# Linear-attention block with a routed FFN row: the kv blocks multiplied by wo on 32x32 tiles of the PE array, in program order

## The chip, the cores and the metric

One core of a Trainium2 chip runs the whole kernel as one launch. The time is device microseconds of that core. The engines are called PE (matmul; its weight loads are listed apart as PEld), DVE (the vector engine), ACT (the activation engine), POOL and SP; SP here only issues DMAs, and POOL does so too.

## What is computed

The input x has 2048 tokens of 1024 numbers. Everything is bf16 in memory.

```python
def _A_ref(x, wqkv, wo):                     # H = 32 heads of Dh = 32
    qkv = (x @ wqkv) ...                     # q, k, v by head
    phi = lambda t: jnp.where(t > 0, t + 1, jnp.exp(t)) + 1e-6
    pq, pk = phi(q), phi(k)
    kv = jnp.einsum("bhsd,bhse->bhde", pk, v)
    z = jnp.einsum("bhsd->bhd", pk)
    num = jnp.einsum("bhqd,bhde->bhqe", pq, kv)
    den = jnp.einsum("bhqd,bhd->bhq", pq, z)[..., None] + 1e-6
    return (num / den) ... @ wo
...
g = _sigmoid((x * gate_w).sum(-1, keepdims=True))
return g * a + (1 - g) * b
```

Here `a` is the attention above. `b` is x, with the output of a gated FFN (1024 to 3584 to 1024) added to the one token with the largest router value. Each head has its own 32x32 block kv, so for four heads (one "group" g of 128 channels) the product pk^T v is a 128x128 matrix of which only the four 32x32 blocks on the diagonal are wanted.

## The kernel before

The kernel has four stages. Sizes are partitions x columns.

- **Loading and first blocks** (lines 128 to 295): x arrives transposed (`xT`), the k and v weights as `wkv`, the q weights as `wq`. POOL writes constants: the identity `ident`, and `mask_bd` (lines 146 to 149), a 128x128 mask that is 1 on the four diagonal blocks.
- **The token loop** (lines 507 to 530), over 16 tiles of 128 tokens. For each tile four units `unit_KV` (line 222) of eight 128x512 matmuls each make k and v, and `unit_KVACC` (line 228) adds pk^T [v, 1] of all eight groups to three PSUM banks `kvacc`; its column 128 is z. Between them stand units of other work, as tables say (lines 33 to 36): units `unit_Q` (line 234), and pieces of the FFN. There are 32 Q units (8 groups g, 4 blocks j of 512 tokens); one is eight 128x512 matmuls into a bank of `ps_work`, which has four banks, and then phi: ACT computes `u`, then `e`, and DVE writes `pq_all` (lines 182 to 193). `Q_PER_T` (line 33) puts 15 Q units into the token loop. The FFN's gate and up weights are multiplied in steps; its down rows are added up on DVE (`yacc`, lines 438 to 443). The loads of the down rows stand between the loads of the second half's gate and up weights (`ffn_pieces`, line 447).
- **The middle** (lines 531 to 622). One Q unit, the last `unit_KVACC`, the end of the FFN (`yps`, `brow`), another Q unit. Then DVE copies z out (`zcol`, `zc`) and multiplies `kvacc` by the mask into `kvbd` (line 546). `den_group(0)` (line 561) makes the denominators of blocks j = 0 and 1 with sixteen 128x32-tile matmuls `dps`, which read `pq_all` of the first 16 Q units; ACT adds epsilon (`dn`), DVE takes the reciprocal (`rd`), and four DMAs, two on SP and two on POOL, spread it to `rdp`. Eight 128x128 transposes turn `kvbd` into `pt`, one DVE copy makes `kvT` of it (lines 604 to 607). A loop (lines 612 to 618) runs the last 14 Q units; after each of the last eight stands `unit_M(g)` (line 596), which multiplies group g's 128x128 `kvT` by wo: two 128x512 matmuls and two ACT copies into `m_sb`. After each Q unit stands one `norm_step` (line 586): DVE copies one row of `rdp` to all partitions (`stream_shuffle` into `rb`, four buffers), and POOL multiplies one 128x512 piece of `pq_all` by it. There are 32 such pieces, eight groups for each block j, in the order of j.
- **The output loop** (lines 625 to 649), over the 16 token tiles t: two banks of eight matmuls each of `pq_all` by `m_sb`, DVE combines them with the gated x (`ot`), a DMA writes the tile. Tile t needs all eight normalised pieces of block j = t // 4. In tile 0 also stands `den_group(1)`, for j = 2 and 3. `NORM_PER_T` (line 37) gives the norm steps after each tile: 2 after tile 0, none after 1 and 2, 3 after each later one until the pieces are used up.

What sets the order: the lines are recorded in the order of the code, and a scheduler then places them on each engine. Where `strict[0]` is true, the helper of line 72 ties each instruction of PE, DVE or ACT to the one before it, so that engine keeps the order of the code. In the kernel before it is false from line 297 on, except for a few lines. All instructions that go through that helper carry line 77 in the profile.

Of the kernel before, what the change touches and what calls it, by code (L numbers as in the profile page):

```python
# [13 lines left out]
BF = mybir.dt.bfloat16  # L14
F32 = mybir.dt.float32
I32 = mybir.dt.int32
U32 = mybir.dt.uint32
ALU = mybir.AluOpType
# [4 lines left out]
P = 128  # L23
S = 2048
D = 1024
# [3 lines left out]
NG = D // P  # L29
EPS = 1e-6  # L30
LN1EPS = math.log1p(EPS)
N_WARM = 6
Q_PER_T = {4: 2, 5: 1, 6: 1, 7: 2, 8: 1, 9: 1, 10: 2, 11: 1, 12: 1, 13: 2, 14: 1, 15: 0}
GU_AFTER = {(6, "end"), (7, 1), (7, "end"), (8, 1), (8, "end"), (9, "end"), (10, "end"), (11, "end")}
DOWN_STEPS = {9: (1, 1, 1, 1), 10: (1, 1, 1, 1), 11: (1, 1, 1, 1), 12: (1, 1, 1, 1, 1), 13: (1, 1, 1, 1), 14: (1, 1, 1, 1), 15: (1, 1, 1)}
FFN_DEPTH = 9
NORM_PER_T = [2, 0, 0, 3, 3, 3, 3, 3, 3, 3, 3, 3, 3, 3, 3, 3]


@with_exitstack  # L40
def kernel(
# [13 lines left out]
    nc = tc.nc  # L55
# [5 lines left out]
    const = ctx.enter_context(tc.tile_pool(name="const", bufs=1))  # L61
# [3 lines left out]
    ps_ffn = ctx.enter_context(tc.tile_pool(name="ps_ffn", bufs=1, space=PSUM))  # L65
# [4 lines left out]
    strict = [True]  # L70

    def in_order(engine, names):
        last = [None]

        def wrap(fn):
            def call(*a, **k):
                inst = fn(*a, **k)  # L77
                if last[0] is not None and strict[0]:
                    tc.add_manual_dep(inst.ins, last[0].ins.name, NOSYNC, reason="program order on this engine")
                last[0] = inst  # L80
                return inst

            return call

        return SimpleNamespace(**{n: wrap(getattr(engine, n)) for n in names})

    pe = in_order(nc.tensor, ["matmul", "transpose"])
    dve = in_order(nc.vector, ["memset", "tensor_copy", "tensor_scalar", "tensor_scalar_add", "tensor_tensor", "scalar_tensor_tensor",
                               "reciprocal", "max", "max_index", "tensor_reduce", "stream_shuffle"])
    sp = in_order(nc.sync, ["dma_start", "dma_start_transpose"])  # L90
    act = in_order(nc.scalar, ["activation", "copy"])
# [4 lines left out]
    kvbd = keep.tile([P, NG, P], BF)  # L96
# [45 lines left out]
    ident = const.tile([P, P], BF)  # L142
    make_identity(nc, ident[:])
    nc.scalar.dma_start(out=wrg_rows[0:8, :], in_=B_w_r.rearrange("(c p) -> c p", p=P))
    nc.scalar.dma_start(out=wrg_rows[8:16, :], in_=gate_w.rearrange("(c p) -> c p", p=P))
    mask_bd = const.tile([P, P], F32)
    nc.gpsimd.memset(mask_bd[:], 0.0)
    for i in range(4):
        nc.gpsimd.memset(mask_bd[32 * i : 32 * i + 32, 32 * i : 32 * i + 32], 1.0)
    nc.gpsimd.memset(mzc[:], 0.0)  # L150
    for hh in range(4):
        for g0 in range(4):
# [39 lines left out]
    def phi_evac(ps, out_ap):  # L192
        phi_dve(ps, phi_exp(ps), out_ap)
# [34 lines left out]
    def unit_KVACC(t):  # L228
        for g in range(NG):
            pe.matmul(kv_slot(g), lhsT=pk_t[t][:, g * P : (g + 1) * P], rhs=vt_t[t][:, g, :],  # L230
                             start=False, stop=False, skip_group_check=True)
        del pk_t[t], vt_t[t]

    def unit_Q(g, j):
        ps = ps_work.tile([P, 512], F32, tag="w")
        for c in range(KC):
            pe.matmul(ps[:], lhsT=wq[:, c, g * P : (g + 1) * P], rhs=xT[:, c, 512 * j : 512 * j + 512],
                             start=(c == 0), stop=(c == KC - 1))
        phi_evac(ps[:], pq_all[:, g, 512 * j : 512 * j + 512])
# [35 lines left out]
    for t in (2, 3):  # L275
        kv_open(t)
        for nb in range(2):
            pool, tag = (ps_t, "t") if t == 2 else (ps_work, "w")
            ps = pool.tile([P, 512], F32, tag=tag)
# [19 lines left out]
    for c in range(KC):  # L299
        for j in range(4):  # L300
            pe.matmul(rps[32 * j : 32 * j + 32, :], lhsT=wrg_pad[:, c, :], rhs=xT[:, c, 512 * j : 512 * j + 512],
                                  start=(c == 0), stop=(c == KC - 1), tile_position=(0, 32 * j))
# [173 lines left out]
    def ffn_step(n):  # L476
        for _ in range(n):
            ffn_flush()
            wt, comp = inflight.popleft()
            comp(wt)  # L480
            ffn_prefetch()
# [3 lines left out]
    def down_step(n):  # L485
        for _ in range(n):
            ffn_flush()
            if down["cur"] is None:
                down["cur"] = inflight.popleft()
            wt, comp = down["cur"]  # L490
            comp(wt, down["n"] % 2)
            if down["n"] % 2:
                down["cur"] = None
                ffn_prefetch()
            down["n"] += 1
# [11 lines left out]
    q_units = deque((g, j) for j in range(4) for g in range(NG))  # L507
    for t in range(4):
        unit_KVACC(t)
    for t in range(4, NT):  # L510
        for nb in range(4):
            unit_KV(t, nb)
            if nb == 1 and t > 4:
                unit_KVACC(t - 1)
            if (t, nb) in GU_AFTER:
                ffn_step(4)
            steps = DOWN_STEPS.get(t, ())
            if nb < len(steps):
                down_step(steps[nb])
        for i in range(Q_PER_T[t]):  # L520
            unit_Q(*q_units.popleft())
# [5 lines left out]
        if t == 5:  # L527
            router_part2()
        if (t, "end") in GU_AFTER:
            ffn_step(4)  # L530
# [2 lines left out]
    down_finish()  # L533
    gates()
    unit_Q(*q_units.popleft())

    zcol = keep.tile([P, NG], F32)
    for i in range(3):
        n = 3 if i < 2 else 2
        acc3 = kvacc[i][:, 0 : 129 * n].rearrange("p (g e) -> p g e", e=129)  # L540
        dve.tensor_copy(zcol[:, 3 * i : 3 * i + n], acc3[:, :, 128])
    dve.tensor_tensor(zc[:], mzc[:], zcol[:].unsqueeze(2).to_broadcast([P, NG, 32]), op=ALU.mult)
    for i in range(3):
        n = 3 if i < 2 else 2
        acc3 = kvacc[i][:, 0 : 129 * n].rearrange("p (g e) -> p g e", e=129)
        dve.tensor_tensor(kvbd[:, 3 * i : 3 * i + n, :], acc3[:, :, 0:128],
                                mask_bd[:].unsqueeze(1).to_broadcast([P, n, P]), op=ALU.mult)
    ph1.close()

    pb = ctx.enter_context(tc.tile_pool(name="pb", bufs=1))  # L550
    m_sb = pb.tile([P, NG, D], BF)
    wo = pb.tile([P, NG, D], BF)
    nc.sync.dma_start(out=wo[:], in_=A_wo.rearrange("(g p) n -> p g n", p=P))
    kvT = pb.tile([P, NG, P], BF)
    rdp = [pb.tile([P, 512], F32, name=f"rdp{i}") for i in range(2)]
    for r in rdp:
        nc.gpsimd.memset(r[:], 1.0)
# [1 line left out]
    ps_den = ctx.enter_context(tc.tile_pool(name="ps_den", bufs=3, space=PSUM))  # L559

    def den_group(pair):
        dps = ps_den.tile([P, 512], F32, tag="d")
        for g0 in range(4):
            for jj in range(2):
                for g1 in range(2):
                    g = 4 * g1 + g0
                    j = 2 * pair + jj
                    q = 2 * jj + g1
                    pe.matmul(dps[32 * q : 32 * q + 32, :], lhsT=zc[:, g, :], rhs=pq_all[:, g, 512 * j : 512 * j + 512],
                                     start=(g0 == 0), stop=(g0 == 3), tile_position=(0, 32 * q))  # L570
        dn = tmpb.tile([P, 512], F32, tag="dn")
        act.activation(dn[:], dps[:], ACTF.Identity, bias=eps_t[:, 0:1])
        rd = tmpb.tile([P, 512], F32, tag="rd")
        dve.reciprocal(rd[:], dn[:])
        for hh in range(4):
            eng = nc.sync if hh % 2 == 0 else nc.gpsimd
            eng.dma_start(out=rdp[pair][32 * hh : 32 * hh + 16, :], in_=rd[hh : P : 8, :])
        return rdp[pair]

# [6 lines left out]
    def norm_step(n):  # L586
        for _ in range(n):
            if not norm_units:
                return
            rd, g, j = norm_units.popleft()  # L590
            rb = tmpb.tile([P, 512], F32, tag="rb", bufs=4)
            dve.stream_shuffle(rb[:], rd[:], [8 * (j % 2) + g] * 32)
            sl = pq_all[:, g, 512 * j : 512 * j + 512]
            nc.gpsimd.tensor_tensor(sl, sl, rb[:], op=ALU.mult)  # L594

    def unit_M(g):
        for nh in range(2):
            ps = ps_den.tile([P, 512], F32, tag="d")
            pe.matmul(ps[:], lhsT=kvT[:, g, :], rhs=wo[:, g, 512 * nh : 512 * nh + 512], start=True, stop=True)
            act.copy(m_sb[:, g, 512 * nh : 512 * nh + 512], ps[:])  # L600

    rdA = den_group(0)
    unit_Q(*q_units.popleft())
    pt = ps_den.tile([P, NG, P], BF, tag="d")
    for g in range(NG):
        pe.transpose(pt[:, g, :], kvbd[:, g, :], ident[:])
    dve.tensor_copy(kvT[:], pt[:])
    normalise(rdA, 0)
    normalise(rdA, 1)
    g_m = 0  # L610
    nq_done = 0
    while q_units:
        unit_Q(*q_units.popleft())
        nq_done += 1
        if g_m < NG and nq_done > 6:
            unit_M(g_m)
            g_m += 1
        norm_step(1)
    while g_m < NG:
        unit_M(g_m)  # L620
        g_m += 1
    phq.close()

    fin = ctx.enter_context(tc.tile_pool(name="fin", bufs=3))
    for t in range(NT):
# [8 lines left out]
        for c0, cw in cols:  # L634
            ps = ps_work.tile([P, 512], F32, tag="w")
            for g in range(NG):
                pe.matmul(ps[:, 0:cw], lhsT=pq_all[:, g, t * P : (t + 1) * P], rhs=m_sb[:, g, c0 : c0 + cw],
                                 start=(g == 0), stop=(g == NG - 1))
# [6 lines left out]
        if t == 0:  # L645
            rdB = den_group(1)
            normalise(rdB, 2)
            normalise(rdB, 3)
        norm_step(NORM_PER_T[t])

# [29 lines left out]
```

## Time and profile before

| | |
|---|---|
| median of 3 runs | 257.94 us (257.4 to 258.1) |
| the profiled execution | 257.94 us, of which 256.4 us are its span |
| granted PE clock | 0.998 |
| PE busy | 249.9 us |
| DVE, ACT, POOL busy | 145.7, 126.9, 47.0 us |

The span is what the profile shows, from the first instruction to the last; 1.54 us of the execution's time lie outside it. A matmul's duration in the profile contains the time in which it passes through the array, and the next one starts before it ends: the 128x512 matmuls last 380 ns each, and start 216 ns after each other. So the cost of a row of matmuls is read from start to start. The profile's stages by time: the token loop ends at 162.8 us, the middle runs to 196.5 us, the output loop to the end.

### The profile page before, as it was taken

To read this page: it belongs to the slowest core of one execution; us is meant where nothing else is said; L and a number is where in the kernel's file an instruction comes from. 1 tells how busy PE (TensorE), PEld (TensorE's weight loads), DVE (VectorE), ACT (ScalarE), POOL (GpSimd) and SP (SyncE) were. 2 spreads that over 40 slices of the span, in tenths; PEclk is the share of its full clock that TensorE was granted. 3 is DMA by queue.
4 is the path that set the end of the run, shared out by engine and by line. 5 is a ranking of instruction groups with operands and counts; after the bars stand their busy time and mean duration, and the time that the engine had idled before them with its cause. 6 is when DMAs were issued, how large, how long until landed. Compare 5 with 4: busy or idle time off the path is not lost.

```text
span 256.4 us, 3781 instructions
## 1 busy us (share of the span) xinstructions
PE 249.9 (97%) x1400; PEld 116.6 (45%) x1426; DVE 145.7 (57%) x238; ACT 126.9 (49%) x202; POOL 47.0 (18%) x99
## 2 busy tenths in 40 slices
PE   8999999999999999999999999999999999999994
PEld 3444454454444444444444444444444444444443
DVE  0055024324155368996899723575986779954443
ACT  2195324545354444654445646466899732352210
POOL 6000001010000000000000000012997029960000
PEclk9999999999999999999999999999999999999999
DMA  6999992007999999879898100077000473454222
GB/s 189 307 330 189 238 315 76 0 3 239 354 348 348 340 336 344 255 227 328 270 438 276 4 0 0 4 234 237 1 3 0 121 233 119 164 179 149 84 82 82
DMA packets 47257, 47.71 MB, mean 186 GB/s; under 512 B 18364, under 2 KB 35140, under 8 KB 47176
## 3 DMA queue, kind: packets, MB, share of 16 engines
q1 hardware_dynamic: 46952, 47.34, 60.3%
q8 instruction: 11, 0.18, 0.3%
q0 software_dynamic: 256, 0.14, 0.2%
q14 instruction: 6, 0.05, 0.1%
q10 hardware_dynamic: 32, 0.00, 0.0%
HBM read 39.34 MB, written 8.40 MB: 186 GB/s over the span
## 4 chain that ended last, share of the span: by engine, by line
PE 95%; DMA 2%; issue 1%; SPq 1%; DVE 0%
PE ps L77 87%; PE kvacc L77 3%; PE first L77 2%; DMA wkv<-in_A_wqkv_dram 2%; PE dps L77 1%; PE rps L77 1%; SPq L77 1%; PE yps L77 0%; DVE ot L77 0%; PE pt L77 0%; PE xs_ps L77 0%; PE hps L77 0%; PE wps L77 0%
## 5 line engine op out<-in xcount | busy, mean ns | idle before, releaser
L77 PE MATMUL ps<-wkv,xT 128*128 128x512 bf16 x467 | 107.2, 380 | 0.6
L77 PEld LDWEIGHTS <-xT 128*128 128x128 bf16 x512 | 48.7, 98 | 58.9 <-issue 4.2
L77 PE MATMUL ps<-xT,wq 128*128 128x512 bf16 x249 | 58.0, 380 | 0.3
L77 ACT ACTIVATE u<-ps 128x512 f32<-128x512 f32 x60 | 35.8, 596 | 40.5 <-PE ps L77 37.2
L77 PE MATMUL ps<-m_sb,pq_all 128*128 128x512 bf16 (+1 forms) x259 | 55.2, 373 | 0.4 <-issue 0.2
L77 ACT ACTIVATE e<-u 128x512 f32<-128x512 f32 x64 | 40.4, 632 | 1.7
L77 PEld LDWEIGHTS <-pq_all 128*128 128x128 bf16 x264 | 25.7, 98 | 29.9 <-issue 0.4
L77 PEld LDWEIGHTS <-wq 128*128 128x128 bf16 x256 | 24.8, 98 | 30.4 <-issue 0.8
L594 POOL TENSOR_TENSOR pq_all<-pq_all,rb 128x512 bf16<-128x512 bf16 x32 | 36.0, 1160 | 8.7 <-DVE rb L77 8.7
L77 DVE SCALAR_TENSOR_TENSOR yacc<-wt,hcol,yacc 128x1024 f32<-128x1024 bf16 x27 | 34.6, 1281 | 3.7 <-DMA wt<-in_B_w_down_dram 3.1
L77 ACT CAST vt<-ps 128x512 bf16<-128x512 f32 x32 | 18.8, 588 | 34.5 <-PE ps L77 34.5
L77 DVE SCALAR_TENSOR_TENSOR pq_all<-ps,e 128x512 bf16<-128x512 f32 x32 | 21.6, 684 | 21.3 <-ACT e L77 21.3
L77 DVE SCALAR_TENSOR_TENSOR ot<-ps,gate,xg 128x512 bf16<-128x512 f32 (+1 forms) x33 | 23.7, 725 | 16.5 <-PE ps L77 15.0
L77 ACT ACTIVATE xg<-xt,omg 128x1024 f32<-128x1024 bf16 x16 | 18.2, 1147 | 25.9 <-DVE ot L77 25.9
L77 DVE SCALAR_TENSOR_TENSOR pk<-ps,e 128x512 bf16<-128x512 f32 x28 | 19.2, 687 | 20.1 <-ACT e L77 20.1
L77 DVE STREAM_SHUFFLE rb<-rdp 128x512 f32<-128x512 f32 x32 | 22.4, 736 | 0.0
L209 POOL MEMSET vt<- 128x8 bf16 x16 | 1.9, 137 | 105.7 <-PE kvacc L77 105.7
L77 PEld LDWEIGHTS <-pk 128*128 128x128 bf16 x128 | 8.5, 98 | 3.3 <-issue 0.4
L77 PE MATMUL kvacc<-vt,pk 128*128 128x129 bf16 x128 | 9.7, 221 | 0.1
L77 ACT CAST m_sb<-ps 128x512 bf16<-128x512 f32 x16 | 9.3, 583 | 0.0
L77 PE MATMUL first<-wkv,xT 128*128 128x512 bf16 x31 | 7.8, 396 | 0.6 <-DMA wkv<-in_A_wqkv_dram 0.6
L77 DVE RECIPROCAL rd<-dn 128x512 f32<-128x512 f32 x2 | 6.7, 3353 | 2.1 <-ACT dn L77 2.1
(96 smaller groups left out, 76.4 us busy)
## 6 DMA issues: line engine op xcount, KB each, us to landing
wt<-in_B_w_down_dram SPq DMA_DIRECT2D x14, 512.0 KB, 5.7
wt<-in_B_w_gate_dram SPq DMA_DIRECT2D x8, 512.0 KB, 7.0
wt<-in_B_w_up_dram SPq DMA_DIRECT2D x8, 512.0 KB, 8.8
xt<-xp SPq DMA_DIRECT2D x16, 256.0 KB, 2.7
out_dram<-ot SPq DMA_DIRECT2D x15, 256.0 KB, 2.0
wt<-in_B_w_gate_dram SPq DMA_DIRECT2D x8, 384.0 KB, 7.6
wt<-in_B_w_up_dram SPq DMA_DIRECT2D x8, 384.0 KB, 7.1
wkv<-in_A_wqkv_dram SPq DMA_DIRECT2D x8, 256.0 KB, 5.0
```

What stands on the lines that cost most here:

```text
L77: inst = fn(*a, **k)
L209: nc.gpsimd.memset(vt_t[t][:, :, 128:129], 1.0)
L594: nc.gpsimd.tensor_tensor(sl, sl, rb[:], op=ALU.mult)
```

## The change

- `Q_PER_T` gives 13 Q units to the token loop and not 15 (one fewer in tile 13, one fewer in tile 14). One more Q unit runs before `den_group(0)`, so that exactly the 16 units that it reads are before it, and the unit that stood right behind it moves into the loop, which now has 16 units.
- The mask goes: `kvbd` is a plain copy of `kvacc`.
- The eight 128x128 transposes become 32 products of one 32x32 block each with the identity (`unit_kvT`), into four banks. Four copies, two on ACT and two on DVE, make `kvT`.
- The sixteen 128x512 matmuls of `unit_M` become four batches of sixteen 32x32-tile matmuls with 512 columns. Row tile r of a batch writes bank r, column tile c its partitions 32c to 32c+31. The sixteen copies into `m_sb` go half to ACT and half to DVE. A batch needs four banks at once (three of `ps_den`, one of `ps_ffn`). The batches stand after units 4, 7, 10 and 13 of the loop.
- wo is loaded by eight DMAs of 32 partitions each, not by one.
- `den_group` and the whole loop are in program order on PE, DVE and ACT.
- The four `rdp` DMAs of `den_group(0)` are all issued by POOL.
- The loop has 8 norm steps and not 14: one after units 5, 6, 8, 9, 11, 12, 14 and 15. The output loop has 2, 3, 3 after tiles 0 to 2, and then 2 after each of tiles 3 to 10.

The lines that load and add the FFN's down rows are the same in both kernels.

```diff
-Q_PER_T = {4: 2, ... 12: 1, 13: 2, 14: 1, 15: 0}
+Q_PER_T = {4: 2, ... 12: 1, 13: 1, 14: 0, 15: 0}
+M_AFTER = {4: (0, 0), 7: (0, 1), 10: (1, 0), 13: (1, 1)}
-NORM_PER_T = [2, 0, 0, 3, 3, 3, 3, 3, 3, 3, 3, 3, 3, 3, 3, 3]
+NORM_PER_T = [2, 3, 3, 2, 2, 2, 2, 2, 2, 2, 2, 0, 0, 0, 0, 0]
...
     unit_Q(*q_units.popleft())
+    unit_Q(*q_units.popleft())
...
-        dve.tensor_tensor(kvbd[:, 3 * i : 3 * i + n, :], acc3[:, :, 0:128],
-                                mask_bd[:].unsqueeze(1).to_broadcast([P, n, P]), op=ALU.mult)
+        dve.tensor_copy(kvbd[:, 3 * i : 3 * i + n, :], acc3[:, :, 0:128])
...
-    nc.sync.dma_start(out=wo[:], in_=A_wo.rearrange("(g p) n -> p g n", p=P))
+    for hf in range(2):
+        for r in range(4):
+            nc.sync.dma_start(out=wo[32 * r : 32 * r + 32, hf, :, :], in_=wo_v[hf, r])
...
     def den_group(pair):
         dps = ps_den.tile([P, 512], F32, tag="d")
+        strict[0] = True
...
+        strict[0] = False
...
-            eng = nc.sync if hh % 2 == 0 else nc.gpsimd
+            eng = nc.sync if pair and hh % 2 == 0 else nc.gpsimd
...
+    def unit_kvT():
+        pt = four_banks("pt")
+        for hf in range(2):
+            for r in range(4):
+                for c in range(4):
+                    pe.matmul(pt[c][32 * r : 32 * r + 32, 32 * hf : 32 * hf + 32],
+                              lhsT=kvbd[32 * c : 32 * c + 32, 4 * hf + r, 32 * c : 32 * c + 32],
+                              rhs=ident[32 * c : 32 * c + 32, 32 * c : 32 * c + 32],
+                              start=True, stop=True, tile_position=(32 * c, 32 * r))
...
+    def unit_M(hf, nh):
+        pm = four_banks("pm")
+        for c in range(4):
+            for r in range(4):
+                pe.matmul(pm[r][32 * c : 32 * c + 32, :], lhsT=kvT[32 * r : 32 * r + 32, hf, c, :],
+                          rhs=wo[32 * r : 32 * r + 32, hf, c, 512 * nh : 512 * nh + 512],
+                          start=True, stop=True, tile_position=(32 * r, 32 * c))
+        for r in range(4):
+            eng = dve.tensor_copy if r % 2 else act.copy
+            eng(m_sb[:, 4 * hf + r, 512 * nh : 512 * nh + 512], pm[r][:])
...
     rdA = den_group(0)
-    unit_Q(*q_units.popleft())
-    pt = ps_den.tile([P, NG, P], BF, tag="d")
-    for g in range(NG):
-        pe.transpose(pt[:, g, :], kvbd[:, g, :], ident[:])
-    dve.tensor_copy(kvT[:], pt[:])
...
+    strict[0] = True
+    for i in range(len(q_units)):
         unit_Q(*q_units.popleft())
-        nq_done += 1
-        if g_m < NG and nq_done > 6:
-            unit_M(g_m)
-            g_m += 1
-        norm_step(1)
...
+        if i == 0:
+            unit_kvT()
+        if i in M_AFTER:
+            unit_M(*M_AFTER[i])
+        elif i >= 5:
+            norm_step(1)
+    strict[0] = False
```

More of the change, by code (lines that the diff above doesn't have):

```diff
@@ L32 @@
 N_WARM = 6
-Q_PER_T = {4: 2, 5: 1, 6: 1, 7: 2, 8: 1, 9: 1, 10: 2, 11: 1, 12: 1, 13: 2, 14: 1, 15: 0}
+Q_PER_T = {4: 2, 5: 1, 6: 1, 7: 2, 8: 1, 9: 1, 10: 2, 11: 1, 12: 1, 13: 1, 14: 0, 15: 0}
 GU_AFTER = {(6, "end"), (7, 1), (7, "end"), (8, 1), (8, "end"), (9, "end"), (10, "end"), (11, "end")}
+M_AFTER = {4: (0, 0), 7: (0, 1), 10: (1, 0), 13: (1, 1)}
 DOWN_STEPS = {9: (1, 1, 1, 1), 10: (1, 1, 1, 1), 11: (1, 1, 1, 1), 12: (1, 1, 1, 1, 1), 13: (1, 1, 1, 1), 14: (1, 1, 1, 1), 15: (1, 1, 1)}
 FFN_DEPTH = 9
-NORM_PER_T = [2, 0, 0, 3, 3, 3, 3, 3, 3, 3, 3, 3, 3, 3, 3, 3]
+NORM_PER_T = [2, 3, 3, 2, 2, 2, 2, 2, 2, 2, 2, 0, 0, 0, 0, 0]
 @with_exitstack
@@ L145 @@
     nc.scalar.dma_start(out=wrg_rows[8:16, :], in_=gate_w.rearrange("(c p) -> c p", p=P))
[L146 to L149, printed above, removed]
     nc.gpsimd.memset(mzc[:], 0.0)
@@ L551 @@
     m_sb = pb.tile([P, NG, D], BF)
-    wo = pb.tile([P, NG, D], BF)
-    nc.sync.dma_start(out=wo[:], in_=A_wo.rearrange("(g p) n -> p g n", p=P))
-    kvT = pb.tile([P, NG, P], BF)
+    wo = pb.tile([P, 2, 4, D], BF)
+    wo_v = A_wo.rearrange("(hf r c e) n -> hf r e c n", hf=2, r=4, c=4)
+    for hf in range(2):
+        for r in range(4):
+            nc.sync.dma_start(out=wo[32 * r : 32 * r + 32, hf, :, :], in_=wo_v[hf, r])
+    kvT = pb.tile([P, 2, 4, 32], BF)
     rdp = [pb.tile([P, 512], F32, name=f"rdp{i}") for i in range(2)]
@@ L594, in norm_step @@
             nc.gpsimd.tensor_tensor(sl, sl, rb[:], op=ALU.mult)
[L596 to L600, printed above, removed]
-    rdA = den_group(0)
-    unit_Q(*q_units.popleft())
-    pt = ps_den.tile([P, NG, P], BF, tag="d")
-    for g in range(NG):
-        pe.transpose(pt[:, g, :], kvbd[:, g, :], ident[:])
@@ L607, with four_banks @@
-    dve.tensor_copy(kvT[:], pt[:])
+    def four_banks(name):
+        banks = [ps_den.tile([P, 512], F32, tag="d", name=f"{name}{r}") for r in range(3)]
+        banks.append(ps_ffn.tile([P, 512], F32, tag="f", name=f"{name}3"))
+        return banks
+    def unit_kvT():
[8 more added lines that the diff above has]
+        for c in range(4):
+            eng = dve.tensor_copy if c % 2 else act.copy
+            eng(kvT[:, :, c, :], pt[c][:, 0:64].rearrange("p (h d) -> p h d", h=2))
@@ new lines, in unit_M @@
+    def unit_M(hf, nh):
+        pm = four_banks("pm")
+        for c in range(4):
+            for r in range(4):
[5 more added lines that the diff above has]
+            eng(m_sb[:, 4 * hf + r, 512 * nh : 512 * nh + 512], pm[r][:])
@@ L608 @@
+    rdA = den_group(0)
     normalise(rdA, 0)
     normalise(rdA, 1)
-    g_m = 0
-    nq_done = 0
-    while q_units:
+    strict[0] = True
+    for i in range(len(q_units)):
         unit_Q(*q_units.popleft())
-        nq_done += 1
-        if g_m < NG and nq_done > 6:
-            unit_M(g_m)
-            g_m += 1
-        norm_step(1)
-    while g_m < NG:
-        unit_M(g_m)
-        g_m += 1
+        if i == 0:
[4 more added lines that the diff above has]
+            norm_step(1)
```

## The prediction

> **What bounds the kernel.** I read the page's busy shares and slices first, then PE's waits, then the chain of work, then the timeline of the middle.
>
> ```profile
> span 256.4 us, 3781 instructions
> ...
> PE 249.9 (97%) x1400; PEld 116.6 (45%) x1426; DVE 145.7 (57%) x238; ACT 126.9 (49%) x202; POOL 47.0 (18%) x99
> ...
> PE   8999999999999999999999999999999999999994
> ```
>
> PE is full in every slice but the first and last. Its waits are three rows, all in the first 8 us or far too small:
>
> ```profile
> PE warm_ps L77 <- PEq L664: 1.0, 1, 1.0
> PE first L77 <- DMA wkv<-in_A_wqkv_dram: 0.6, 2, 0.3
> PE ps L77 <- issue: 0.2, 1, 0.2
> ```
>
> So the time is PE's instructions laid end to end. A change can win only by taking work from PE, and loses every wait that it gives PE. The chain in order of time has what the changed pieces cost PE (columns: start, us, what):
>
> ```profile
> 58.17 0.30 PE xs_ps L77 x9
> ...
> 167.09 0.97 PE dps L77 x16
> 168.06 0.54 PE ps L77 x2
> 168.60 0.45 PE pt L77 x8
> ```
>
> `pt` is the eight transposes, 56 ns each. `xs_ps` is nine tiny products, each with its own weight load: 33 ns apiece, the fastest pace of such pairs here. `dps`, on 128x32 tiles, runs at about 57 ns: four column tiles share a stream of 216 ns. The sixteen `ps<-wo,kvT` matmuls cost 16 x 0.216 = 3.46 us.
>
> What a Q unit needs after its last matmul is seen in the timeline of the middle (start, duration, engine):
>
> ```profile
> 174.26 0.60 ACT L77 ACTIVATE u<-ps 128x512 f32<-128x512 f32 x1 [0.47 <-PE ps L77]
> 174.89 0.63 ACT L77 ACTIVATE e<-u 128x512 f32<-128x512 f32 x1
> 175.55 0.69 DVE L77 SCALAR_TENSOR_TENSOR pq_all<-ps,e 128x512 bf16<-128x512 f32 x1 [0.95 <-ACT e L77]
> ...
> 177.93 0.73 DVE L77 STREAM_SHUFFLE rb<-rdp 128x512 f32<-128x512 f32 x1
> ...
> 178.82 2.29 POOL L594 TENSOR_TENSOR pq_all<-pq_all,rb 128x512 bf16<-128x512 bf16 x2 [4.96 <-DVE rb L77]
> ```
>
> u starts 0.20 after the unit's end (matmuls from 194.35 plus 8 x 0.216 give 196.08; the u there starts at 196.28). With 0.60, 0.63, 0.69 and the gaps, `pq_all` is written **2.2 us** after PE has finished the unit. A normalisation takes 0.73 on DVE, 0.16 of hand-over and 1.15 on POOL: about **2.0 us** more. Before, all of this is hidden.
>
> **The change, part by part.** The sum is made against the profiled execution, 257.94 us (span 256.4 plus 1.54 outside); that is also the median.
>
> *Moved Q units.* 2 x 1.73 us leave the token loop and come back in the middle: 0. DVE's last `yacc` ends at 144.9, 18 us before `yps`, and PE there has four banks, so an earlier tile 14 (by 1.73) meets DVE free. 0 (up to +0.5 if DVE were still behind).
>
> *Mask.* `kvbd` copies instead of products (0.52 and 0.41 us on DVE) stay hidden behind two Q units: 0. POOL's five mask memsets lie in its first 4 us; PE's first transposes wait for x: 0.
>
> *Down rows.* The built order of SP's loads is the same in both kernels: 0.
>
> *wo in eight DMAs.* Before, one DMA is issued at 166.84, 3.45 after the last `kvacc`, and lands in 9.9 us. Eight issues of about 0.4 to 0.6 us take 4 us; the first batch stands 16 us after that `kvacc`. About 3 us of margin even if it all lands at 3.45 + 9.9: 0. Without the margin each us late is a us on PE.
>
> *rdp by POOL.* Four issues of 0.5 us and 3.9 us to landing: about 6 us after `rd`. The first shuffle stands behind the sixth unit's phi, about 10 us after `rd`: 0.
>
> *Order, first place: `dps`.* Before, the scheduler put `dps` 14 matmuls behind the 16 units that it reads. Now it follows unit 16 at once, in program order, and its sixteenth matmul reads that unit's `pq_all`. With U the end of unit 16: `pq_all` at U + 2.2; PE has done 15 `dps` at U + 0.09 + 15 x 0.0575 = U + 0.95. Behind the waiting matmul the whole loop queues on PE. **+1.25 us** (0.9 to 1.6).
>
> *Second place: the last normalisations of j = 0.* Before, block 0's eight pieces were done six units before the loop's end. Now the steps after units 14 and 15 are the last two, and in program order each shuffle stands behind its unit's phi. With T the end of the last Q unit: piece 6 is shuffled from T - 1.73 + 2.2 = T + 0.45, and is through POOL at T + 2.5, at PE by T + 2.6. In the built order PE has seven matmuls of tile 0 (six pieces, one of the second bank) ahead: T + 1.5. **+1.1 us** (0.7 to 1.6). Piece 7 is ready at T + 2.2 + 2.0 + 0.1 = T + 4.3; PE, delayed, has eight more matmuls to do first: 2.6 + 1.73 = T + 4.35. So 0 more.
>
> *Third place: j = 1 at tile 4.* Before, 14 of the 16 pieces of j = 0 and 1 were through in the loop; now 8, and tile 4's last three are shuffled only behind tile 2's `ot`. DVE, in the built order: two `ot` and one shuffle until T + 6.9, the reciprocal (3.35 us in its row) until T + 10.2, two `ot` (0.74) and two shuffles until T + 12.9, two `ot` until T + 14.3, then three shuffles (0.65 apart) ending at 15.0, 15.7, 16.3. POOL needs 1.15 for each: 16.35, 17.5, 18.65. PE: tile 0 and `dps` until T + 5.95, 15 matmuls of tile 1 until 9.2, tiles 2 and 3 (3.46 each) until 16.1; piece 7 of tile 4 is wanted at 17.6, and comes at 18.75. **+1.15 us** (0.4 to 1.8). Later blocks have four tiles for eight pieces at two a tile: 0.
>
> *Products.* A batch at the pace of `xs_ps` is 16 x 0.033 = 0.53, and about 0.2 for changing tile shape (around `dps` PE loses 0.09 ahead and 0.06 to 0.28 behind). 4 x 0.73 = 2.9 for 3.46: **-0.55**. Bounds: all sixteen together, 4 x (0.216 + 0.15) = 1.5: -2.0; at the pace of `dps`, 64 x 0.0575 + 0.8 = 4.5: +1.0; no two row tiles together, 64 x 0.216 = 13.8: +10.4. No row here has a row tile. I take the issue pace: with both tilings the 216 ns stream is shared by up to sixteen, and something under 57 ns then sets the pace. The copies go half to DVE, which then has 5 x 0.69 + 2 x 0.74 = 4.9 us of work in each 5.9 us of loop (three units and a batch): 0.
>
> *Blocks turned.* 32 x 0.033 + 0.2 = 1.25 for 0.45: **+0.8** (0 to +1.7). The copies are wanted four units later.
>
> The Trainium skill speaks of these products, beside the numbers above. "TensorE: Matmul & The Clock Gate", Measured speedup vs the span model, gives 660 ns for sixteen 32x32 tiles of 512 columns: an estimate from that page is 2.64 us for the four batches, which would make the sum 0.26 lower. Against the change speaks "TensorEngine Tiling (Array Packing)", Key Properties: "Changing tiling mode (not just tile) drains the TensorE". The gaps around `dps` agree in kind, at 0.06 to 0.28 us; the change makes ten such switches more, and no run here shows them for row tiles.
>
> **Sum.** 1.25 + 1.1 + 1.15 - 0.55 + 0.8 = +3.75: **261.7 us**. The work taken from PE is small; the waits that program order and the later normalisation give it are not.
>
> **Rivals.**
>
> - *The row tiles run all at once* (faster). Place: the four batches. Price: -2.0 (and the blocks turned at +0.3). It decides only if the three waits sum to under 0.9 us; with 0.6 it gives 257.94 - 1.7 + 0.6 = 256.8. For it: 512 columns are one stream however many tiles share it, as `dps` shows for four. Against: the waits are in the built order itself, 3.5 us by the rows above. With its products and waits at their low ends (2.0) the time is 258.2. Chance of faster by over 0.3%: 0.09.
> - *It moves little* (the down rows aren't changed; what PE gains it gives back): within 0.3%, 257.2 to 258.7. Needs waits of about 2 us with the cheapest products. Chance 0.11.
> - *Row tiles run one after another* (much slower): +10.4 instead of -0.55: 272.6. For it: consecutive products of a batch share a column tile, and nothing here shows row tiles overlapping. Against: nothing shows them excluding each other. Chance 0.05.
> - *wo comes late.* The first two batches need its first half, 12.5 us after issue at the latest. At the pace before it lands in 5; at a quarter of that pace in 20, 7 us late: about 269. For it: each DMA now writes 32 partitions. Against: the rows that it moves are the same 2 KB. Chance 0.04.
> - The forecast, slower by 1 to 7 us: 0.71.
>
> 0.3% (0.77 us) is about what this kernel's measurement can tell from no change. Faster 0.09, within 0.11, slower 0.80. The range leaves out the last two rivals above and the faster one below: all low ends give +0.3 (258.2), the high ends without it 1.6 + 1.6 + 1.8 + 1.0 + 1.7 = +7.7; I take 258.0 to 265.0.
>
> **What would show it.** PE's waits gain rows: `dps` for DVE `pq_all` (about 1.25 us, once), a weight load of `pq_all` for POOL at tile 0 (1.1) and at tile 4 (1.15). `pm` costs about 0.7 us a batch, start to start, `pt` 1.25. It would be wrong if PE shows no such waits, if a batch is near 0.35 or over 1.2 us, or if PE waits for wo.

## The result, and the profile after

The changed kernel takes **259.44 us** (median of 4 runs, 259.17 to 259.56) against 257.88 before (257.4 to 258.1): a ratio of **1.0061**, interval 1.0044 to 1.0079. That is slower by 1.56 us, where +3.75 was forecast. The profiled execution took 259.56 us; 258.0 of it are its span (256.4 before), at a granted clock of 1.0.

Of the page: the span, the busy times, and PE's forty slices.

```profile
span 258.0 us, 3927 instructions
...
PE 248.5 (96%) x1471; PEld 114.7 (44%) x1498; DVE 150.4 (58%) x247; ACT 124.2 (48%) x196; POOL 47.7 (18%) x96
...
PE   7999999999999999999999999899998999999994
```

PE has 1.4 us less to do, and the span is 1.6 us longer. Two slices in the middle, near 165 and 197 us, have fallen from 9 to 8. PE's waits (columns: us in total, times, the longest) say why:

```profile
PE ps L78 <- POOL pq_all L596: 1.2, 2, 0.7
PE dps L78 <- DVE pq_all L78: 1.1, 1, 1.1
PE warm_ps L78 <- PEq L682: 1.0, 1, 1.0
PE first L78 <- DMA wkv<-in_A_wqkv_dram: 0.8, 1, 0.8
PE ps L78 <- issue: 0.3, 2, 0.2
```

The last three rows were there before, of about the same size. The first two are new. The weight loads have a new row as well, 2.5 us at the same two stops: a weight load stops first, and the matmul behind it is then late by the rest.

```profile
PEld L78 <- POOL pq_all L596: 2.5, 3, 1.2
```

PE's timeline of the middle (start, duration, what, the idle time before it) has all the changed pieces:

```profile
159.94 0.64 PE L78 MATMUL yps<-yacc,ones_f 128*32 128x256 f32 x8
160.74 3.40 PE L78 MATMUL ps<-xT,wq 128*128 128x512 bf16 x15 [0.16 <-issue]
164.07 1.04 PE L78 MATMUL dps<-pq_all,zc 128*32 128x512 bf16 x15
166.21 0.38 PE L78 MATMUL dps<-pq_all,zc 128*32 128x512 bf16 x1 [1.10 <-DVE pq_all L78]
166.52 1.90 PE L78 MATMUL ps<-xT,wq 128*128 128x512 bf16 x8
168.35 0.29 PE L78 MATMUL pt<-ident,kvbd 32*32 32x32 bf16 x32
168.81 6.85 PE L78 MATMUL ps<-xT,wq 128*128 128x512 bf16 x31 [0.16 <-issue]
175.59 0.43 PE L78 MATMUL pm<-wo,kvT 32*32 32x512 bf16 x16
175.96 5.35 PE L78 MATMUL ps<-xT,wq 128*128 128x512 bf16 x23
```

Fifteen `dps` start right behind the sixteenth Q unit; the sixteenth `dps` is held up for 1.10 us, and all of the loop stands behind it. A batch of sixteen products lies between 175.59 and the next Q unit's start at 175.96: **0.37 us**. (31 and 23 records where 32 and 24 matmuls ran: a record is missing in each, so the gap at 168.81 is a matmul without a record; the `issue` rows of PE's waits, here and before, are such gaps.) The start of the output loop, and its later stop:

```profile
196.37 1.67 PE L78 MATMUL ps<-m_sb,pq_all 128*128 128x512 bf16 x7
198.77 2.17 PE L78 MATMUL ps<-m_sb,pq_all 128*128 128x512 bf16 x9 [0.73 <-POOL pq_all L596]
201.09 1.05 PE L78 MATMUL dps<-pq_all,zc 128*32 128x512 bf16 x16
202.07 11.83 PE L78 MATMUL ps<-m_sb,pq_all 128*128 128x512 bf16 x53
214.35 40.12 PE L78 MATMUL ps<-m_sb,pq_all 128*128 128x512 bf16 x190 [0.45 <-POOL pq_all L596]
```

Both stops are on the chain that ended last (columns: start, us, what); before, this stretch of the chain was PE alone, but for some 0.2 us of issue, most of it a matmul without a record:

```profile
195.47 0.64 ACT e L78
...
196.14 0.63 DVE pq_all L78
196.77 0.72 DVE rb L78
...
197.55 1.17 POOL pq_all L596
...
198.77 2.19 PE ps L78 x9
```

It is the path that the prediction described for the second place: phi of the last but one unit, its shuffle, POOL's product, and then PE.

**Where the time went.** Start to start on PE, profile against profile:

| stage | before | after | difference | forecast |
|---|---|---|---|---|
| start of `yps`, less the two Q units moved (3.46) | 163.32 | 159.94 | +0.08 | 0 |
| `dps` start to next Q unit | 0.98 | 2.45 | +1.47 | +1.25 |
| blocks turned, with the change of tile shape | 0.45 | 0.33 | -0.12 | +0.8 |
| products with wo: 16 x 0.216; 4 x (0.37 + 0.10) | 3.45 | 1.88 | -1.57 | -0.55 |
| tile 0 to `dps` (after has one matmul more, 0.22) | 3.55 | 4.72 | +0.95 | +1.1 |
| second `dps` to the next matmul (before: from 200.06 to 201.04, see below) | 0.98 | 0.98 | 0 | 0 |
| from there to the last matmul (after has one matmul fewer, 0.22) | 52.00 | 52.42 | +0.64 | +1.15 |
| behind the last matmul | | | +0.15 | 0 |

The sum is +1.60, the difference of the spans. The 0.10 is what PE loses ahead of the smaller tiles: the eight Q matmuls from 166.52 end their starts at 168.25, and `pt` begins at 168.35. For the two rows on the second `dps` the profile before needs care:

```profile
201.26 51.77 PE L77 MATMUL ps<-m_sb,pq_all 128*128 128x512 bf16 x243 [0.16 <-issue]
```

Here 243 records stand for 248 matmuls, and the gap ahead of them is one without a record: it started 0.22 earlier, at 201.04. In the run with both mends, below, all 248 have records, and the first starts 0.98 after `dps`, as in the kernel after.

### The profile page after: what moved, and what is told of

Same layout as the page of the kernel before. It is cut to its first block, busy times and chain, and to the rows that moved or that the text cites. A ratio compares the mean times of both kernels' runs of the same rounds, so it can differ in the third digit from the quotient of the medians.

```text
span 258.0 us, 3927 instructions
## 1 busy us (share of the span) xinstructions
PE 248.5 (96%) x1471; PEld 114.7 (44%) x1498; DVE 150.4 (58%) x247; ACT 124.2 (48%) x196; POOL 47.7 (18%) x96
## 4 chain that ended last, share of the span: by engine, by line
PE 90%; DMA 2%; ACT 2%; POOL 1%; issue 1%; DVE 1%; SPq 0%
PE ps L78 82%; PE kvacc L78 3%; PE first L78 2%; DMA xnat<-in_A_x_dram 2%; POOL pq_all L596 1%; ACT e L78 1%; PE rps L78 1%; ACT u L78 1%; DVE rb L78 1%; PE dps L78 1%; DVE pq_all L78 1%; SPq L78 0%; PE pm L78 0%; ACT m_sb L78 0%; PE pst L78 0%
## 5 line engine op out<-in xcount | busy, mean ns | idle before, releaser
L78 PE MATMUL ps<-xT,wq 128*128 128x512 bf16 x250 | 57.4, 379 | 0.5 <-issue 0.3
L78 DVE CAST r_bf<-rps 128x512 bf16<-128x512 f32 x1 | 0.7, 692 | 12.1 <-PE rps L78 12.1
L78 PE MATMUL ps<-wt,xs_pad 128*32 128x512 bf16 (+1 forms) x128 | 7.5, 355 | 0.0
```

## The experiments

**The theory after the result:** the waits are as forecast, in their places and near their sizes (3.06 us together), and stand in the order and in the number of norm steps, not in the tiles; the tiles give 1.7 us. (The expectations below have 0.86 us for the third wait. That is 0.22 too much, the matmul without a record.) **The rival:** the tiles give little, and the waits are smaller than their rows suggest because something else of the change pays for them (the two moved Q units, the order). If the first holds, each wait must go when its own cause is mended, and the tiles must cost 1.7 us when they are taken back. The first seven runs below and the last change the kernel after; the four between them put the tile products into the kernel before.

### One more Q unit ahead of the first dps

```diff
+    strict[0] = True
+    unit_Q(*q_units.popleft())
     rdA = den_group(0)
...
-    for i in range(len(q_units)):
-        unit_Q(*q_units.popleft())
-        if i == 0:
+    for i in range(16):
+        if i:
+            unit_Q(*q_units.popleft())
+        if i == 1:
             unit_kvT()
```

> One Q unit is moved ahead of dps (17 and not 16 before it), and the turning of the blocks behind the next one; all else as in the changed kernel. Theory (the change loses time in three waits of PE, 1.47 us at dps, 0.95 at tile 0, 0.86 at tile 4): the dps wait goes, 259.4 - 1.4 = 258.0. Rival (the middle is bound by DVE and ACT, so that PE waits somewhere else instead): 259.2 to 259.6, with a new wait in the loop. Rival (program order itself costs): 259.4, no row changes but the one.

Measured: **258.17 us**, ratio to before 0.9999 (0.9982 to 1.0017). The `dps` row is gone from PE's waits, the POOL row is as it was:

```profile
PE ps L78 <- POOL pq_all L596: 1.2, 2, 0.7
PE warm_ps L78 <- PEq L685: 1.0, 1, 1.0
PE first L78 <- DMA wkv<-in_A_wqkv_dram: 0.7, 1, 0.7
```

So the first place is worth 1.3 us by the medians (259.44 less 258.17), and it is the distance between the last phi and its reader. The output loop does not change with it: from tile 0 to PE's end it takes 58.1 us in both.

### A norm step after every unit from the sixth on

```diff
         if i in M_AFTER:
             unit_M(*M_AFTER[i])
-        elif i >= 5:
+        if i >= 5:
             norm_step(1)
```

> Three more norm steps in the loop (after each unit from 5 on, so 11 and not 8); all else as in the changed kernel. Theory of the three waits: piece 7 of block 0 is through three units before the loop's end, and block 1 has three pieces more done by then, so both waits for POOL go: 259.4 - 0.95 - 0.86 = 257.6. Rival (DVE cannot take three more shuffles of 0.73 us in the loop): PE waits for a bank in the loop, 259 or more.

Measured: **257.69 us**, ratio 0.9998 (0.9976 to 1.002). With eleven norm steps in the loop, not eight, POOL is no longer among what PE waits for; the `dps` row stays:

```profile
PE dps L78 <- DVE pq_all L78: 1.1, 1, 1.1
PE warm_ps L78 <- PEq L682: 1.0, 1, 1.0
PE first L78 <- DMA wkv<-in_A_wqkv_dram: 0.6, 1, 0.6
```

The second and the third place are worth 1.75 us together by the medians (1.59 in the table), and both go with three norm steps more in the loop, those that the change leaves out after a batch. This run doesn't part the two.

### Both mends

The edits of the last two runs together.

> Both edits: 17 units ahead of dps and 11 norm steps in the loop. Theory of the three waits: all of 3.3 us goes, and what is left of the change is its products (1.7 us saved): 256.2, ratio 0.993 to the kernel before. Rival (the waits only move): above 257.5.

Measured: **255.95 us**, ratio **0.9922** (0.9902 to 0.9943): faster than both kernels. One row of PE's waits is left, and the slices are full again:

```profile
PE   8999999999999999999999999999999999999994
```
```profile
PE warm_ps L78 <- PEq L685: 1.0, 1, 1.0
```

The tile products do make this kernel faster, by about the 1.7 us of the table (the interval is 1.5 to 2.5), once nothing is made to wait for their sake.

### The changed order, with whole tiles

```diff
-        for c in range(4):
-            for r in range(4):
-                pe.matmul(pm[r][32 * c : 32 * c + 32, :], ... tile_position=(32 * r, 32 * c))
+        for r in range(4):
+            g = 4 * hf + r
+            pe.matmul(pm[r][:], lhsT=kvT[:, g, :], rhs=wo[:, g, 512 * nh : 512 * nh + 512], start=True, stop=True)
```

The 128x128 transposes, the mask and the single DMA of wo are back as well.

> The changed kernel with whole products in place of the tile products: eight 128x128 transposes, four batches of four 128x512 matmuls, the mask, wo in one DMA; order, Q units and norm steps as in the changed kernel. Theory (tile products save 1.7 us): 259.4 + 1.7 = 261.1. By the prediction's pace of 33 ns: 259.2. If tile batches cost PE more around them than in them: below 260.

Measured: **261.55 us**, ratio 1.0133 (1.0104 to 1.0162), 2.1 us more than the kernel after by the medians. Its profile has a wait of 0.8 us for a gate weight DMA in the token loop, which the kernel after lacks, so the stage is the better measure: from the Q unit behind `dps` to tile 0 it takes 31.54 us (167.09 to 198.63), and the kernel after 29.85 (166.52 to 196.37). The difference, **1.69 us**, is the table's -1.57 and -0.12. Both new waits are there unchanged (1.2 and 1.1 us), so the tiles have no part in them.

### 32 more block products, all on one tile

```diff
+        for _ in range(16):
+            for hf in range(2):
+                pe.matmul(pt[0][0:32, 32 * hf : 32 * hf + 32], lhsT=kvbd[0:32, 4 * hf, 0:32],
+                          rhs=ident[0:32, 0:32], start=True, stop=True, tile_position=(0, 0))
```

> The changed kernel with 32 block products more, all on tile (0, 0), writing the same two blocks again and again; the output is the same. If the pace belongs to issue (what the prediction took, from the tiny products at 33 ns): 32 more cost the same as the first 32, 0.2 to 0.5 us. If products overlap only on different tiles: 33 ns or more each, 1 us or more.

One execution, 260.47 us. The stage of the blocks on PE:

```profile
168.35 1.16 PE L78 MATMUL pt<-ident,kvbd 32*32 32x32 bf16 x64
169.44 7.08 PE L78 MATMUL ps<-xT,wq 128*128 128x512 bf16 x32
```

The 64 take 1.09 us from start to start, where the 32 alone take 0.23 (next run). The 32 added ones on the one tile cost 0.86, **27 ns each**; the 32 that go round the sixteen tiles cost **7 ns each**. It is being on different tiles that makes them cheap, as far as this run can tell: the added ones also write one bank, where the 32 write four. The next run keeps the four banks and changes the row tiles alone.

### All products on one row of tiles

```diff
-                pe.matmul(pm[r][32 * c : 32 * c + 32, :], lhsT=kvT[32 * r : 32 * r + 32, hf, c, :],
-                          rhs=wo[32 * r : 32 * r + 32, hf, c, 512 * nh : 512 * nh + 512],
-                          start=True, stop=True, tile_position=(32 * r, 32 * c))
+                pe.matmul(pm[r][32 * c : 32 * c + 32, :], lhsT=kvT[0:32, hf, c, :],
+                          rhs=wo[0:32, hf, c, 512 * nh : 512 * nh + 512],
+                          start=True, stop=True, tile_position=(0, 32 * c))
```

> The changed kernel with all products of wo on row tile 0 (four column tiles): each batch multiplies the first 32 partitions only, so the product with wo is not the reference's. If rows of tiles overlap as columns do in the batches of 0.37 us, four column tiles alone take 4 x 216 = 0.86 us a batch and 54 ns a product, as dps does: +2.0 us, 261.4. If issue set the pace: no change, 259.4.

One execution, 264.01 us; 1.86 of them are a token loop that ended later (`yps` at 161.80) and have nothing to do with the edit.

```profile
170.21 0.29 PE L78 MATMUL pt<-ident,kvbd 32*32 32x32 bf16 x32
170.44 7.08 PE L78 MATMUL ps<-xT,wq 128*128 128x512 bf16 x32
177.45 1.07 PE L78 MATMUL pm<-wo,kvT 32*32 32x512 bf16 x16
178.45 4.92 PE L78 MATMUL ps<-xT,wq 128*128 128x512 bf16 x22
```

A batch now takes 1.00 us and not 0.37. Four column tiles share a stream (16 products in 1.00 is 62 ns each, near the 57 of `dps`), and in the kernel after four row tiles share it once more. The four batches would cost 2.5 us more on one row: the row tiles are what makes the change pay.

### Without program order

```diff
-        strict[0] = True
...
-        strict[0] = False
...
-    strict[0] = True
     for i in range(len(q_units)):
```

> The changed kernel without program order in the loop and in the two den_groups; all else as in it. Left free, the scheduler puts five matmuls ahead of the last dps, and 16 shuffles (not 8) among the loop's units. Theory of the three waits, with program order as what holds them: the two waits at tiles 0 and 4 go (1.8 us) and some 1.1 of the 1.47 us at dps: 259.4 - 2.9 = 256.5. Rival (the numbers of norm steps in the code hold the waits, not program order): 258.3, the dps wait alone. Rival (a free order does as badly as with the tile products alone): 264.

Measured: **260.38 us**, ratio 1.0099 (1.0074 to 1.0124): a miss. The scheduler does put other matmuls ahead of the waiting `dps`, and POOL's pieces come in time. But it also places the first shuffle right behind the phi at 174.15, ahead of `rdp`'s landing. DVE's timeline:

```profile
174.15 0.69 DVE L78 SCALAR_TENSOR_TENSOR pq_all<-ps,e 128x512 bf16<-128x512 f32 x1 [1.04 <-ACT e L78]
178.87 0.01 DVE L78 LOAD_MASK_SELECT rb<-rdp  x1 [4.03 <-DMA rdp<-rd]
178.90 0.73 DVE L78 STREAM_SHUFFLE rb<-rdp 128x512 f32<-128x512 f32 x1
179.52 0.68 DVE L78 CAST m_sb<-pm 128x512 bf16<-128x512 f32 x1
```

DVE stands 4.03 us for `rdp`, and the copies of the first batch, which DVE shares now, stand behind the shuffle. So the next batch finds its banks full (PE's waits):

```profile
PE pm L78 <- DVE m_sb L78: 1.9, 2, 1.8
```

The waits that the theory named are gone, at `dps` and at both tiles. Against them stand these 1.9 us, and a second cost: the free order splits each batch in two (12 and 4 products, or 3 and 13, with Q matmuls between), and each half has its own change of shape. The first batch takes 0.35 and 0.33 us where a whole one takes 0.37, with 0.10 ahead of each half; four such batches cost some 1.6 us.

For the wait there are two causes to choose from: DVE held by the first shuffle, or DVE with too much work (16 shuffles in this loop, 8 in the kernel after). The last run below goes to this question.

### The tile products alone, in the kernel before

```diff
-        if g_m < NG and nq_done > 6:
-            unit_M(g_m)
+        if nq_done == 1:
+            unit_kvT()
+        if nq_done in (7, 9, 11, 13):
+            unit_M(g_m // 2, g_m % 2)
             g_m += 1
```

`unit_kvT`, `unit_M` and the eight DMAs of wo are those of the change; the Q units, the mask, the fourteen norm steps and the free order are those of before.

> The kernel before with the tile products alone (32 block products and four batches of sixteen, wo in eight DMAs); order free, Q units, mask and norm steps as before. Theory (batches of 0.37 us and 0.08 ahead, for 3.46 us of whole matmuls): 257.9 - 1.7 = 256.2. By the prediction's pace of 33 ns a product: 258.1. If the tile products need program order or the moved units to pay: 257.5 or more.

Measured: **264.64 us**, ratio 1.0258 (1.0234 to 1.0282): a miss by 8 us, and not by the products, whose whole batches take 0.37 here too (one of the four is split). The scheduler now puts the first shuffle behind the phi of eleven units, at 192.99 on DVE. POOL has nothing to do until then (idle for 20.02 us, for which the row names the PE), and the output loop waits for it piece by piece:

```profile
193.87 15.76 POOL L597 TENSOR_TENSOR pq_all<-pq_all,rb 128x512 bf16<-128x512 bf16 x14 [20.02 <-PE pm L77]
```
```profile
PE ps L77 <- POOL pq_all L597: 3.1, 5, 0.7
...
PE ps L77 <- DVE ot L77: 0.8, 1, 0.8
```

The rows of waits don't show all of the cost. Behind the first stops PE's granted clock is 0.50, from 199 to 205 us, where it is 1.0 before them; eight matmuls from 200.69 take 3.53 us and not 1.73.

### The same, with rdp's DMAs all on POOL

```diff
-            eng = nc.sync if hh % 2 == 0 else nc.gpsimd
+            eng = nc.sync if pair and hh % 2 == 0 else nc.gpsimd
```

> The kernel before with the tile products, as in e8_tiles, and with the four rdp DMAs of den_group(0) issued by POOL as in the changed kernel; order free. In e8_tiles, behind eight wo DMAs on SP, the scheduler put the first shuffle behind eleven units' phi; now it stands behind five. Theory (the 6.6 us of e8_tiles are the late shuffles alone): 258.0 - 1.7 = 256.3. Rival (the free order of the batches, split 12 and 4, or the copies on DVE cost it): 260 or more.

Measured: **263.39 us**, ratio 1.0212 (1.0187 to 1.0238): a miss again. This small edit turns the order over: the first shuffle comes early, DVE stands until `rdp` lands at 180.94, and PE waits 2.7 us for DVE's phi and 0.8 for its `m_sb`. Two of the batches are split, and behind the wait of 2.7 us the granted clock is 0.50 from 185 to 188 us: the sixteen matmuls there take 5.23 us, the next sixteen 3.56.

### The same as the tile products alone, in program order

```diff
+    strict[0] = True
     while q_units:
...
+    strict[0] = False
```

> The kernel before with the tile products, as in e8_tiles, and with the loop in program order on PE, DVE and ACT; rdp still two on SP and two on POOL, 14 norm steps in the loop. Theory (late shuffles cost e8_tiles its time; program order is another cure): 256.3, or up to 1 us more, because the first shuffle now stands behind three phi only and holds DVE until rdp lands. Rival (program order costs by itself): 259 or more.

Measured: **261.82 us**, ratio 1.0165 (1.0129 to 1.02): a third miss, and the plainest. In program order the first shuffle stands behind the phi of the loop's first unit. DVE is held there until `rdp` has landed; meanwhile PE fills the four banks of the Q units, and then waits for a phi to empty one (DVE's timeline, and PE's waits):

```profile
179.65 0.01 DVE L77 LOAD_MASK_SELECT rb<-rdp  x1 [6.14 <-DMA rdp<-rd]
```
```profile
PE ps L77 <- DVE pq_all L77: 3.6, 1, 3.6
```

Here too the stop costs more than its row. The granted clock is 0.50 from 182 to 184 us, and the sixteen matmuls behind the stop take 5.23 us to the next batch, where the sixteen behind that batch take 3.56, 1.67 less:

```profile
181.02 5.30 PE L77 MATMUL ps<-xT,wq 128*128 128x512 bf16 x16 [3.61 <-DVE pq_all L77]
```

With the tiles' -1.69, the stop and the slow matmuls give 256.4 - 1.69 + 3.61 + 1.67 = 260.0, and the span is 260.1. So the products cost no more here; the hold costs it all.

### The same, with norm steps only from the sixth unit on

```diff
-        norm_step(1)
+        if nq_done > 5:
+            norm_step(1)
...
-NORM_PER_T = [2, 0, 0, 3, 3, 3, 3, 3, 3, 3, 3, 3, 3, 3, 3, 3]
+NORM_PER_T = [2, 3, 3, 2, 2, 2, 2, 2, 2, 2, 2, 0, 0, 0, 0, 0]
```

The output loop makes up for the steps left out, with the numbers of the kernel after.

> Before with the tile products, its fourteen Q units in the loop in program order, and the norm steps only after the units from the sixth on (9 of them in the loop, the first shuffle behind six units' phi). If VectorE was what the three former tries ran into (it held for rdp's landing, then had more work than TensorE), its work here is 14 x 0.69 + 8 x 0.68 + 9 x 0.67 + 3.7 = 24.8 us in TensorE's 26.6, and the first shuffle comes after rdp has landed: about 256.2, up to 257.2 because in the units 7 to 14 it needs 4.1 us for each two units' 3.83 us of TensorE; no wait of TensorE over 1.5 us for pq_all or m_sb in the loop. If the tile products cost something else in this place (or need the two moved Q units), 258.0 or more, with the waits of the former tries still there.

Measured: **257.96 us**, ratio 0.9985 (0.9968 to 1.0003), span 256.4. No wait is left in the loop, so DVE was it, by its hold or by its load (this edit takes away the hold and five of fourteen steps); yet 256.2 to 257.2 was expected. The steps now end late for tile 0: its eighth piece is shuffled at 195.94, when PE has begun the tile at 194.83:

```profile
194.83 1.67 PE L77 MATMUL ps<-m_sb,pq_all 128*128 128x512 bf16 x7
198.02 2.12 PE L77 MATMUL ps<-m_sb,pq_all 128*128 128x512 bf16 x9 [1.52 <-POOL pq_all L597]
200.07 1.05 PE L77 MATMUL dps<-pq_all,zc 128*32 128x512 bf16 x16
```

From tile 0 to `dps` PE takes 5.24 us here and took 3.55 before: 1.69 more. That is just what the tiles gained, and the span is before's to the tenth. The tile products cost the same wherever they stand; they did not need the moved Q units for that.

### Both mends, with sixteen norm steps in the loop

```diff
-        elif i >= 5:
-            norm_step(1)
+        if i >= 5:
+            norm_step(2 if i >= 11 else 1)
...
-NORM_PER_T = [2, 3, 3, 2, 2, 2, 2, 2, 2, 2, 2, 0, 0, 0, 0, 0]
+NORM_PER_T = [0, 0, 3, 2, 2, 2, 2, 2, 2, 2, 2, 0, 0, 0, 0, 0]
```

The edit of the first run, one more Q unit ahead of `dps`, is in it as well.

> The kernel with both mends (one more Q unit ahead of the first den products; norm steps from the fifth unit on), but with 16 norm steps in the loop in place of 11: two after each of the units from the eleventh on. If VectorE is the second bound of the loop, from the sixth unit on it has 11 x 0.69 + 8 x 0.68 + 16 x 0.67 = 23.7 us of work in TensorE's 11 x 1.73 + 4 x 0.45 = 20.8: 1 to 2.5 us slower than the kernel with both mends, that is 257.0 to 258.5, with waits of TensorE for m_sb, pq_all or GpSimd's pieces behind it. If TensorE alone bounds the loop and VectorE takes the five more shuffles beside it: 255.95, the same as with 11.

Measured: **256.29 us**, ratio 0.9939 (0.9917 to 0.9961). The interval overlaps that of eleven steps (0.9902 to 0.9943), the spans are 253.9 and 254.0, and PE's waits show nothing of DVE or POOL. The theory that DVE's load is a second bound of the loop fails. From 164 to 196.5 us DVE is busy for 27.12 of 32.50 us (26.18 with eleven steps), and it falls behind: the loop's last phi starts 3.0 us after PE has gone on to the output loop (193.83).

```profile
196.86 0.67 DVE L78 SCALAR_TENSOR_TENSOR pq_all<-ps,e 128x512 bf16<-128x512 f32 x1
```

But that phi belongs to the last block of tokens, which the output loop reads much later. Being behind costs nothing there; being held long ahead of phi and copies that PE's banks depend on does. With 16 shuffles PE has no wait when DVE is held 0.92 us for the landing, as here, and waits 1.9 us when DVE is held 4.03 us, as in the run without program order. (That run's free order differs as well, so the two are not parted by the hold alone.)

## Why the prediction was wrong in its size

**The three waits: right.** `dps` was forecast at +1.25 and measured +1.47 (the wait is 1.10; the sixteenth matmul, alone behind it, takes 0.31 to the next start, where four that share a stream take 0.22). Tile 0: +1.1, measured +0.95. Tile 4: +1.15, measured +0.64. Together 3.5 and 3.06, in the places, on the engines and for the reasons given; the first goes when its cause is mended, and the other two when theirs is.

**The step that failed** is the mis-sized term of the products: "I take the issue pace". 33 ns apiece came from `xs_ps`, nine products of one shape, 1x128, in one place on the array. A batch was put at 0.53 and 0.2 for the change of shape, 0.73 in all; it takes 0.37 and 0.10. That makes -1.57 for -0.55. The step put 16 products at 33 ns each; 0.37 is one stream of 0.216 and 0.15 more for all sixteen. The same pace made the blocks turned +0.8, and they measured -0.12: 32 x 33 ns where 32 x 7 ns stand. These two terms are 1.94 of the 2.15 us by which the sum is off; the waits are 0.44 of it, and 0.23 of small rows go the other way. The condition "wrong if a batch is near 0.35" named it.

The pace that I took is near right for products on one tile, as the added ones on one tile show with 27 ns. The Trainium skill, in "TensorE: Matmul & The Clock Gate", Wait — 56ns, not 53.3ns?, states that start to start never falls below about 25 ns however few the columns; the 27 ns agree, and the 7 ns of the products that go round sixteen tiles do not, so the rule holds for one tile only. The same page's Measured speedup vs the span model, which the prediction weighed, gives 660 ns for sixteen tiles; a batch here takes 0.43 us from its first start to its last end, and 0.37 to the next instruction's start. Here the measurements decide.

**Changing the tile shape** was taken at 0.2 and measured at 0.10 ahead of the small tiles; what it costs behind them is inside the 0.37. "TensorEngine Tiling (Array Packing)", Key Properties, which speaks of a drain, agrees in kind; ahead of the five groups it is 0.5 us in all, too little to decide.

**The rivals.** "The row tiles run all at once" had -1.7 for products and blocks, and -1.69 was measured; that the sums agree so well is luck, since its parts were -2.0 and +0.3, and -1.57 and -0.12 were measured. Its condition, waits under 0.9 us, was not met. The truth took the rival's price and nearly the forecast's waits: 257.94 - 1.7 + 3.1 and 0.2 of small rows give 259.5. I had tied the cheap products to small waits when nothing links the two. Row tiles one after another: no, they overlap. wo late: no, its eight DMAs were issued by 167.95 and took 5.7 us each (median), and PE never waits for wo.

**Costed at nothing:** the moved Q units (+0.08), the mask, the down rows and the half of the copies on DVE, rightly. The last rests on a condition that the prediction names only for `rdp`: the first shuffle behind its landing. That a shuffle ahead of it would hold the copies and phi, and so PE, the prediction does not say. Three runs that broke it by 4.0 to 6.1 us lost 1.9 to 3.6 us of PE to waits for DVE, and two of them 1.7 us more at the lower clock. The change kept it by starting the norm steps late, with less margin than was thought: the landing was put at about 6 us after `rd`, and in the run with both mends DVE still stands for it 8.6 us after (170.18 to 178.78). The change's first shuffle comes 9.1 us after.

Open stays how many norm steps fourteen units in the loop could take; two a unit there was not tried.

## What to carry to other kernels

Price packed tile products by the stream that they share, and only products on the same tile by their issue pace. When work is put in program order, look for each reader that follows its producer at once and put one unit between the two (worth 1.3 us here), and keep the steps that feed the next stage going: three steps left out of a loop cost about what the tiles gained (1.6 to 1.75 us for 1.7). On an engine in order, an instruction that waits for a DMA goes behind the landing, since what it holds up is not only its own consumer but whatever frees the banks: a hold of 0.9 or 1.3 us cost nothing here, holds of 4.0 to 6.1 us cost PE 1.9 to 3.6. A lag in work that is read late costs nothing.

## What was not expected of the hardware

- Sixteen 32x32 products of 512 columns take 0.37 us from the first one's start to the next instruction's, against 1.00 on one row of tiles: row tiles and column tiles share a stream alike.
- Products of 32 columns start every 7 ns when they go round sixteen tiles, every 27 ns on one tile.
- The change of tile shape costs 0.10 us ahead of the small tiles, and what comes behind them is small enough to hide in the 0.37.
- Behind stops of 2.7 and 3.6 us PE's granted clock was 0.50 for some 3 us, and sixteen matmuls took 5.23 us in place of 3.56; behind single stops of 1.5 and 1.8 us it stayed at 1.0. What PE lost at the long stops was about half as much again as their rows of waits say.
